# Loading the first group's wq and wo from GpSimd instead of SyncE in a decode-attention and gated-MLP forward and backward kernel

## The chip, the cores and the metric

The kernel runs on one core of one Trainium2 chip. The metric is the device time of one launch in microseconds (us): the median of three runs of the kernel before is 722.63 us (722.57 to 722.94). 0.2% of that is 1.45 us. The profile was taken in another execution, of 722.74 us, whose recorded span is 721.0 us; times below are counted from the start of that span.

The engines are named as in the profile: PE (matrix products; PEld its weight loads), DVE (vector), ACT (scalar), POOL (GpSimd) and SP (SyncE, which only issues transfers here). A small q behind a name (SPq, POOLq) is that engine's own instruction queue.

## The reference

One token x of 640 features is normalised and goes through two branches that are added to it: attention over 32 heads of 128 with a cache of 8192 keys and values per head, and a gated MLP of width 1728. The kernel returns the output and the gradients of x, both caches and all five weight matrices. The arithmetic is light; the caches and their gradients are not.

```python
q = xn @ wq                                    # 32 heads of 128
p = softmax(q . k * 128 ** -0.5);  o = p . v   # per head, 8192 positions
out = x + o @ wo + (silu(xn @ w1) * (xn @ w3)) @ w2
# and, for grad_out: d x, d k_cache, d v_cache, d wq, d wo, d w1, d w3, d w2
```

For one query, the gradient of V of a head is an outer product of the probabilities and a row of `grad_out @ wo.T`, and that of K an outer product of the score gradients and q. So each head reads 2 MB of K and 2 MB of V and writes as much back.

## The kernel before, in words

**Slots.** Ten SBUF buffers of 2 MB (`free_slots`) hold the caches. K and V of a head are loaded into two of them, PE transposes the data (L402), ACT copies the transposes out of PSUM (L404), PE forms scores (L423) and weighted sums (L517), and DVE overwrites the buffer in place with the gradient (L550, two halves of 2.28 us each). SP then stores it (`store`, L561 to L567), returns the buffer to the list and calls `load_next` (L137), which issues the next pending K or V load on SP. From L176 on it does so only when three buffers are in the list, so that a load goes into a buffer whose store was issued two stores earlier. Four of the ten buffers hold the MLP's weights until the MLP has run, between heads 1 and 2 (L910 to L913).

**Order.** The scheduling is manual: every engine runs its instructions in the order in which the program emits them, and waits on semaphores. All K and V traffic and the loads of the MLP's weights lie in SP's queue (q1 in the profile); transfers that GpSimd issues lie in another (q0). The two queues share the same 16 DMA engines.

**Groups.** Four heads share a group of weights: `wq_g` (640 rows of 512 columns, 640 KB; 1 KB runs) and `wo_g` (512 rows of 640, 640 KB; 1280-byte runs). Groups 1 and 2 are loaded by GpSimd after heads 0 and 1 (L915 to L917), the later ones after an older group is finished (L615). Only group 0 is loaded by SP (L145, L147), ahead of K and V of head 0.

**What needs group 0.** After the layer norm (L242 to L252), `prep_q(0)` (L279) multiplies xn with `wq_g` on PE (L283), ACT scales the row (L286), PE and ACT turn it into a column (`prep_qc`, L288 to L294), and `first_half` (L303) spreads it into the weight tile `qz` (L307 to L314). On PE the first transposes of head 0 (`T(0,"K",0)`, L903) stand behind these, and what forms scores needs `qz`. DVE reduces `wo_g` against `grad_out` in four steps (`prep_do`, L271 to L277), which `first_do` (L316) takes up in the middle of head 0, behind all transposes of K and two of V. The layer norm itself needs constants that DVE derives from `ident_f`, the identity that GpSimd makes at L179 (`make_identity`); the first of them, `ident_bf` at L181, stands ahead of the others in DVE's order.

**MLP.** At L910 the outer products of head 1 and then `mlp()` run. It stores its weight gradients through GpSimd (L705 to L757) and gives its buffers back; loads of K and V of heads 5 and 6 go into them, so these loads wait for GpSimd's stores.

Of the kernel before, what the change touches and what calls it, by code (L numbers as in the profile page):

```python
# [21 lines left out]
def kernel(  # L22
# [22 lines left out]
    nc = tc.nc  # L45
# [71 lines left out]
    def load_wq(g, eng):  # L117
        wq_g = wpool.tile([P, NC, GW], BF16, name="wq_g", tag="wq_g")
        eng.dma_start(wq_g[:], wq_v[:, :, g * GW:(g + 1) * GW])
        grp[g] = dict(wq=wq_g)  # L120

    def load_wo(g, eng):
        wo_g = wpool.tile([P, GH, D], BF16, name="wo_g", tag="wo_g")
        eng.dma_start(wo_g[:], wo_v[:, g * GH:(g + 1) * GH, :])
        grp[g]["wo"] = wo_g

    def load_group(g, eng):
        load_wq(g, eng)
        load_wo(g, eng)
# [7 lines left out]
    def load_next():  # L137
        if not pending or len(free_slots) < lag[0]:
            return
        kind, h = pending.pop(0)  # L140
        t = free_slots.pop(0)
        (fifo if h == 0 else fifo_wide)(t[:], (kc if kind == "K" else vc)[h])
        kv_tiles[(kind, h)] = t

    load_wq(0, nc.sync)  # L145
    load_next()
    load_wo(0, nc.sync)  # L147
    for _ in range(3):
        load_next()
    mC = free_slots.pop(0)  # L150
    mD = free_slots.pop(0)
# [836 lines left out]
```

## Time and profile before

| | |
|---|---|
| median of 3 runs | 722.63 us (722.57 to 722.94) |
| the profiled execution | 722.74 us, span 721.0 us |
| moved by DMA | 303.55 MB, mean 421 GB/s |
| read, written in HBM | 151.34 MB, 152.91 MB |
| SP's queue (q1), GpSimd's queue (q0) | 276.39 MB, 26.31 MB |
| busy: PE, PEld | 602.7 us, 378.1 us |
| busy: DVE, ACT, POOL | 471.9 us, 365.0 us, 86.0 us |
| mean granted PE clock | 0.93 |

Busy time is the sum of what an engine's instructions took. A row of the timeline gives start, duration, engine, source line, operation, output and inputs, and in brackets how long the engine was idle before it and what ended that. A row of a table by windows gives for each stretch its length, the busy time and number of instructions of each engine, then the granted PE clock, the mean busy share of the DMA engines (a little over 1 where two packets overlap, since a packet counts where it starts) and the rate. A row of the waits gives the waiting engine and line, what released it, the total, the number of waits and the longest. The chain of waits goes back from the last instruction to whatever released each step.

### The profile page before, as it was taken

To read this page: it belongs to the slowest core of one execution; us is meant where nothing else is said; L and a number is where in the kernel's file an instruction comes from. 1 tells how busy PE (TensorE), PEld (TensorE's weight loads), DVE (VectorE), ACT (ScalarE), POOL (GpSimd) and SP (SyncE) were. 2 spreads that over 40 slices of the span, in tenths; PEclk is the share of its full clock that TensorE was granted. 3 is DMA by queue.
4 is the path that set the end of the run, shared out by engine and by line. 5 is a ranking of instruction groups with operands and counts; after the bars stand their busy time and mean duration, and the time that the engine had idled before them with its cause. 6 is when DMAs were issued, how large, how long until landed. Compare 5 with 4: busy or idle time off the path is not lost.

```text
span 721.0 us, 13224 instructions
## 1 busy us (share of the span) xinstructions
PE 602.7 (84%) x5244; PEld 378.1 (52%) x5244; DVE 471.9 (65%) x895; ACT 365.0 (51%) x726; POOL 86.0 (12%) x86
## 2 busy tenths in 40 slices
PE   6989699987999989978986899878988889978931
PEld 4557566645565556545554565445554555545510
DVE  4369927678858886767745765556765666667581
ACT  3641166653566566545554556445654456545510
POOL 0110100000001112111121211111201101111110
PEclk9987999998999999999999999899998999999965
DMA  9999999999999999999999999999999999999996
GB/s 355 405 414 418 436 435 414 430 436 423 422 430 423 429 431 424 421 433 430 423 423 426 427 430 431 418 428 428 437 417 428 429 428 430 427 432 425 427 430 290
DMA packets 23163, 303.55 MB, mean 421 GB/s; under 512 B 3814, under 2 KB 5164, under 8 KB 9916
## 3 DMA queue, kind: packets, MB, share of 16 engines
q1 hardware_dynamic: 16600, 276.39, 90.1%
q0 software_dynamic: 6496, 26.31, 9.1%
q8 instruction: 41, 0.67, 0.4%
q14 instruction: 22, 0.18, 0.1%
q10 hardware_dynamic: 4, 0.00, 0.0%
HBM read 151.34 MB, written 152.91 MB: 422 GB/s over the span
## 4 chain that ended last, share of the span: by engine, by line
DMA 43%; PE 40%; DVE 10%; ACT 3%; issue 2%; SPq 0%; ACTq 0%; DVEq 0%
DMA kv<-in_A_k_cache_dram 24%; PE pT L402 19%; DMA kv<-in_A_v_cache_dram 14%; PE sA L423 5%; DVE kv L550 4%; PE dA L423 4%; DMA out_dram<-kv 4%; PE X L517 4%; PE m L440 2%; ACT KT L404 2%; DMA out_dram<-rel,rel_idx 1%; PE gu_ps L644 1%; PE dh_ps L655 1%; PE pT L283 1%; PE dx_acc L742 1%
## 5 line engine op out<-in xcount | busy, mean ns | idle before, releaser
L404 ACT COPY KT<-pT 128x512 f32<-128x512 f32 x512 | 288.5, 588 | 234.6 <-PE pT L402 212.7
L402 PE MATMUL pT<-ident_f,kv 128*128 128x128 f32 x2048 | 305.9, 288 | 54.3 <-DMA kv<-in_A_k_cache_dram 42.2
L402 PEld LDWEIGHTS pT<-ident_f,kv 128*128 128x128 f32 x2048 | 235.2, 148 | 144.2 <-PE pT L402 53.3
L550 DVE TENSOR_TENSOR kv<-qd,U 128x4096 bf16<-128x4096 bf16 x64 | 146.0, 2283 | 0.0
L550 DVE TENSOR_TENSOR kv<-qd,P 128x4096 bf16<-128x4096 bf16 x64 | 143.6, 2284 | 0.0
L517 PE MATMUL X<-kv,Z 128*32 128x512 bf16 x1024 | 97.0, 414 | 1.8 <-DVE Z L534 1.8
L423 PE MATMUL dA<-KT,qz 128*32 128x512 bf16 x512 | 85.3, 413 | 0.0
L423 PE MATMUL sA<-KT,qz 128*32 128x512 bf16 x512 | 81.5, 398 | 0.0
L370 POOL DMA_INDIRECT out_dram<-wq_g,row_idx x30 | 43.7, 1458 | 286.1 <-DMA out_dram<-wq_g,row_idx 110.4
L500 DVE SCALAR_TENSOR_TENSOR U<-m,P 128x64 bf16<-128x64 f32 x32 | 7.5, 234 | 98.8 <-PE m L440 98.8
L517 PEld LDWEIGHTS <-Z 128*32 128x32 bf16 x1024 | 33.1, 102 | 36.6 <-issue 10.4
L423 PEld LDWEIGHTS <-qz 128*32 128x32 bf16 x1024 | 29.5, 95 | 41.2 <-issue 38.4
L440 PE MATMUL m<-selc,KT 64*128 64x64 f32 x256 | 29.9, 238 | 7.5 <-ACT KT L430 7.5
L440 PEld LDWEIGHTS m<-selc,KT 64*128 64x128 f32 x256 | 21.0, 140 | 28.7 <-ACT KT L430 19.2
L370 POOL DMA_INDIRECT out_dram<-rel,rel_idx x12 | 15.5, 1292 | 138.6 <-DVE rel L596 47.6
L466 DVE TENSOR_REDUCE mrow<-m 128x1 f32<-128x64 f32 x32 | 7.1, 222 | 37.5 <-PE m L440 37.3
L460 ACT CAST qd<-pT 128x256 bf16<-128x256 f32 x32 | 11.9, 373 | 38.2 <-DVE kv L550 30.4
L473 DVE TENSOR_REDUCE negM<-m 128x1 f32<-128x128 f32 x32 | 9.3, 291 | 32.2 <-PE m L470 32.2
L274 DVE SCALAR_TENSOR_TENSOR side<-wo_g,g_bc 128x640 bf16<-128x640 bf16 x32 | 26.2, 819 | 2.3 <-DMA wo_g<-in_A_wo_dram 2.0
L602 DVE SCALAR_TENSOR_TENSOR wq_g<-wq_g,side 128x512 bf16<-128x512 bf16 x40 | 27.3, 682 | 0.0
L532 DVE SCALAR_TENSOR_TENSOR U<-m,P 128x128 bf16<-128x128 f32 x32 | 11.4, 355 | 15.8 <-PE m L530 15.8
L430 ACT COPY KT<-dA 64x512 f32<-64x512 f32 x32 | 18.6, 581 | 5.0 <-PE dA L423 5.0
(179 smaller groups left out, 403.0 us busy)
## 6 DMA issues: line engine op xcount, KB each, us to landing
out_dram<-kv SPq DMA_DIRECT2D x64, 2048.0 KB, 29.8
kv<-in_A_k_cache_dram SPq DMA_DIRECT2D x32, 2048.0 KB, 26.6
kv<-in_A_v_cache_dram SPq DMA_DIRECT2D x32, 2048.0 KB
out_dram<-wo_g POOLq DMA_DIRECT2D x8, 640.0 KB, 15.3
wq_g<-in_A_wq_dram POOLq DMA_DIRECT2D x7, 640.0 KB, 15.7
wo_g<-in_A_wo_dram POOLq DMA_DIRECT2D x7, 640.0 KB, 22.5
kv<-in_B_w_dram SPq DMA_DIRECT2D x2, 1728.0 KB
out_dram<-kv POOLq DMA_DIRECT2D x2, 1728.0 KB, 30.7
```

Of the source, the lines that this page charges most:

```text
L274: nc.vector.scalar_tensor_tensor(junk[:], G_["wo"][:, hh, :], 1.0, g_bc[:], ALU.mult, ALU.mult, accum_out=G_["do"][:, hh:hh + 1])
L370: nc.gpsimd.indirect_dma_start(dwq_row, bass.IndirectOffsetOnAxis(ap=idx, axis=0), src, None, element_offset=g * GW, bounds_check=(D - 1) ...
L402: nc.tensor.transpose(pT[:, k * P:(k + 1) * P], W3[:, 4 * c + k, :], ident_f[:])
L404: nc.scalar.copy(KT[:].rearrange("p k w -> p (k w)"), pT[:])
L423: nc.tensor.matmul(S_[kind][q:q + QW, :], lhsT=S_["qz"][:, o:o + QW], rhs=KTb[c][:, par, :], start=(c0 == 0 and par == 0), stop=(c0 == NCH ...
L430: nc.scalar.copy(XS[0:QH].rearrange("p k w -> p (k w)"), S_.pop(kind)[0:QH, :])
L440: nc.tensor.matmul(S_["m"][:, b0:b0 + 4 * J].rearrange("p (x c k t) -> p k x c t", x=4, k=4, t=2)[:, k], lhsT=XS[0:QH, k, :], rhs=selc[0:Q ...
L460: nc.scalar.copy(qd[:].rearrange("p a d -> p (a d)"), hd[h].pop("ps_r"))
L517: nc.tensor.matmul(xg["X"][q:q + QW, :], lhsT=Z[:, o:o + QW], rhs=W[:, N4 * i:N4 * (i + 1)], start=(slot == 0 and i < 4), stop=(slot == NS ...
L532: nc.vector.scalar_tensor_tensor(S_["U2"][:], S_["V"][:, 0:J].unsqueeze(2).to_broadcast([P, J, 2]), S_["m"][:, OC + NS:OC + NS + 1], S_["P ...
L550: nc.vector.tensor_tensor(dst[:, lo * DH:hi * DH].rearrange("p (j a b) -> p j a b", a=DH // 2, b=2), vec.rearrange("p (a b) -> p a b", b=2 ...
L602: nc.vector.scalar_tensor_tensor(wq_g[:, ci, :], wq_g[:, ci, :], 1.0, dqb, ALU.mult, ALU.mult, accum_out=dxa[:, ci, g:g + 1])
```

## The change

The loads of group 0 go from SP's queue to GpSimd's, and are GpSimd's first instructions, ahead of `make_identity`. SP begins with K and V of heads 0 and 1. Nothing else is changed; the same bytes are loaded into the same tiles.

```diff
-    load_wq(0, nc.sync)
-    load_next()
-    load_wo(0, nc.sync)
-    for _ in range(3):
+    load_group(0, nc.gpsimd)
+    for _ in range(4):
         load_next()
```

In the built programs SP has 139 instructions in place of 141 and POOL 65 in place of 63; PE, DVE and ACT have the same instructions in the same order.

## The prediction

> **What bounds the kernel now.** I read the page's slices and queues first, then the chain of waits, then what SP waits for.
>
> ```profile
> DMA  9999999999999999999999999999999999999996
> GB/s 355 405 414 418 436 435 414 430 436 423 422 430 423 429 431 424 421 433 430 423 423 426 427 430 431 418 428 428 437 417 428 429 428 430 427 432 425 427 430 290
> ...
> q1 hardware_dynamic: 16600, 276.39, 90.1%
> q0 software_dynamic: 6496, 26.31, 9.1%
> ...
> DMA 43%; PE 40%; DVE 10%; ACT 3%; issue 2%; SPq 0%; ACTq 0%; DVEq 0%
> ```
>
> The DMA engines are busy in every slice, and the two queues' packets fill 90.1 + 9.1 = 99.2% of the span. The same bytes can't be moved in much less time, so the kernel is bound by transfers. The chain of waits seems to disagree, with half of it on PE and DVE. In order of time it runs through PE and DVE from 12.01 to about 300 us and through transfers afterwards. So until 300 us PE never waits for data, and the early stages decide whether a late PE is felt. SP's waits tell:
>
> ```profile
> SPq L111 <- DMA out_dram<-kv: 485.8, 56, 14.1
> SPq L106 <- DVE kv L550: 72.6, 14, 10.5
> ```
>
> SP's loads wait for stores to land, which is the DMA waiting for itself, six times longer than its stores wait for DVE. A store of 2,048 KB lands 29.8 us after its issue (median, table of issues), while moving it takes 2.097 MB / 425 GB/s = 4.9 us: some 25 us of other work lies ahead of it. That queue is the cover for anything that makes the engines late.
>
> The start, by windows of 1 us (the last two columns are DMA share and GB/s) and by timeline:
>
> ```profile
> 2.00:3.00 1.00, 0.37 (x6) 0.29 (x6) 0.79 (x4) 0.82 (x1) 0.00 (x0) 1.00 0.72 228
> 3.00:4.00 1.00, 0.57 (x2) 0.48 (x2) 0.36 (x3) 0.00 (x0) 0.00 (x0) 1.00 1.01 313
> 4.00:5.00 1.00, 0.59 (x2) 0.50 (x2) 0.03 (x2) 0.26 (x1) 0.00 (x0) 1.00 1.07 338
> ...
> 6.80 2.29 PE L283 MATMUL pT<-wq_g,xn_col_bf 128*128 128x512 bf16 x5 [2.12 <-DMA wq_g<-in_A_wq_dram]
> ...
> 12.01 3.60 PE L402 MATMUL pT<-ident_f,kv 128*128 128x128 f32 x16 [0.90 <-DMA kv<-in_A_k_cache_dram]
> 13.58 0.82 DVE L274 SCALAR_TENSOR_TENSOR side<-wo_g,g_bc 128x640 bf16<-128x640 bf16 x1 [1.99 <-DMA wo_g<-in_A_wo_dram]
> ```
>
> Transfers begin a little after 2 us. wq, alone in the queue, lands 6.0 us after its issue and PE starts on it at 6.80; K of head 0 arrives at 12.0 and wo at 13.6.
>
> **The change, part by part.**
>
> 1. *The weights arrive later.* The loads of wq and wo that POOL already issues for groups 1 and 2 are the nearest rows. Up to 130 us the three loads of wq_g take 6.0 / 10.8 / 15.7 us to land (min, median, max; the 6.0 is SP's), and POOL's two of wo_g 15.2 and 21.3. All of POOL's share the engines with a full SP queue, as the changed ones will. POOL would issue wq at 0.74 us, where its identity begins now, and wo 1.05 us later (the length of POOL's first such issue). So wq lands at 0.74 + 10.8 = 11.5 to 0.74 + 15.7 = 16.4, and wo at 1.79 + 15.2 = 17.0 to 1.79 + 21.3 = 23.1; with the page's median for all seven loads of wo, 22.5, at 24.3. I take wq at 12.5: it lies nearer the 10.8, which went beside MLP weights in packets of about 14 KB, since K and V of head 0 go in 16 KB packets, and the 15.7 partly beside 32 KB ones.
>
> The Trainium skill ("DMA: Bandwidth & Descriptors", Queues, rings and completion order) says that each DMA engine takes turns between its queues, packet by packet. The trace agrees: the same 640 KB take 6.0 us alone and 10.8 beside a full queue. Another rule of that page (Anatomy of one DMA) gives a GpSimd transfer 2.0 us and its bytes at 436 GB/s; as an estimate from that page, wq would take 3.5 us and land at 4.2. By that rule the first point costs nothing, the next cover being point 2. The rows of 10.8 and 15.7 speak against it; it holds for a queue without rivals.
>
> 2. *The identity comes later.* POOL's issues took 1.05 and 0.79 us, so everything on DVE behind L181 and the layer norm shift by 1.8 us: its last step goes from 5.53 to 7.4 us. wq at 11.5 or later hides that. Without this cover PE would start on wq at 7.6 instead of 6.80, which K's arrival at 12.0 still hides but for a few tenths.
>
> 3. *Head 0 starts later.* From PE's start on wq (6.80) to the end of the L307 products (11.11) is 4.3 us of dependent steps, then the transposes follow. With wq at 12.5 they start at 16.8 in place of 12.0: 4.8 us late. Bounds: 11.5 + 4.3 = 15.8, so 3.8; 16.4 + 4.3 = 20.7, so 8.7. wo needs 3.6 us more on DVE (13.58 to 17.22) before `first_do`, which PE reaches at 20.84 now and at 25.6 then. With wo at 17.0 to 23.1 DVE is done at 20.6 to 26.7, so this adds at most 1.1; with 24.3, 27.9 - 20.84 = 7.1 in all. I take 5 us, within 3.8 to 8.7. Behind PE everything of heads 0 and 1 and of the MLP is late by this: stores, POOL's gated loads of groups 1 and 2, and the MLP's stores.
>
> 4. *What the lateness costs: nothing, under this cover.* The first store (V of head 0) is issued at 37.09 and lands at 67.1, where the next load waits for it. At that moment the stores of K (46.15) and V of head 1 (53.34) are the queue; they land at 72.7 and 79.2, as the next two loads, issued at 72.67 and 79.19, show. A store issued 15 us later would still find the queue full. The tightest place comes later. The load at 123.97 (K of head 6) waits for POOL's last big MLP store, issued at 87.63. SP's queue then holds V's load of head 5 and V's store of head 2 (110.34), which land at about 127 and 131.7 by the trace's landings. A load's first bytes move about 1.5 us after its issue (0.74 to 2.2 at the start). So this load may be 131.7 - 124.0 - 1.5 = 6.2 us late before SP's queue runs dry. The 5 us are inside. Later, from 130 to 230 us, SP's stores wait for DVE 28.8 us in all, but the DMA share by windows of 5 us stays at 0.93 or more, so the queue isn't dry there either; after 230 the stores find DVE done (0.8 us).
>
> 5. *What the transfers gain.* Now 640 KB in 1 KB runs move at 313 and 338 GB/s (3 to 5 us) against some 425 in the long run: (425 - 313) + (425 - 338) = 199 KB, 0.47 us; from 2.28 to 3.0, 306 - 228 = 78 KB, 0.18 us; around wo (9 to 13 us: 286, 379, 543, 379) 113 KB, 0.27 us. Sum 0.9 us at most, if K and V run at the full rate there. Against it: where POOL's loads of group 1 mix with SP's queue, 30 to 45 us, the rates are 417, 398 and 383, mean 399, a loss of up to 15 x 26 = 390 KB, 0.9 us; with group 2 (50 to 70 us) 415, some loss too, partly of other origin. So 0 to 0.9 gained; I take the middle, 0.5 us.
>
> **Sum.** 722.74 - 0.5 + 0 = 722.2 us for an execution such as the profiled one. Its 722.74 are the span of 721.0 and 1.7 around it, and lie 0.1 above the median of 722.63, so this is 0.1% below. A difference under 0.2%, 1.45 us, is about what a measurement can't tell from no change.
>
> **Rivals.**
>
> - *The lateness outlasts the queue* (slower). Place: the load of K of head 6 behind POOL's MLP store. It decides from 6.2 us of lateness; the price is what lies above. At the upper bound of 8.7 it is 2.5 us: 722.2 + 2.5 = 724.7. For: 15.7 is the median over POOL's seven loads of wq. Against: once SP's queue is dry, the store it waits for gets the engines alone and lands sooner. Chance 0.10.
> - *Engines set the pace after all* (slower). If the chain of waits is right up to 300 us, nothing absorbs the 5 us: 722.7 + 5 = 727.7. For: 40% of that chain on PE. Against: DMA at 9 in every slice. Chance 0.10.
> - *The transfers gain more* (faster). From 25 to 30 us the rate is 338, a shortfall of 5 x 87 = 435 KB, 1.0 us. If two queues keep the engines fed there too, the gain is 0.9 + 1.0 = 1.9: 720.8. Against: POOL's queue is empty again by then. Chance 0.13.
> - *No cost and no gain beyond noise*: my forecast, 722.2, own range 721.2 to 723.6. Chance 0.67.
>
> The range takes in the faster rival and the first slower one with its bounds, 720.7 to 725.2; the second slower one stays out. Faster by over 0.2%: 0.13; within: 0.67; slower: 0.20.
>
> **What would show it.** Of the profile after: PE's first row of L283 at 11.5 to 16.4 us and the first transposes 4.3 later, with the layer norm done before; the first store issued about 42 instead of 37; the load behind it still at 67; DMA shares near 1 around 125 to 135 us; the chain in transfers at the end. The prediction is wrong if the DMA share sinks below 0.9 between 40 and 140 us, or if the lateness at the first store is still there in the last one (issued at 696.3 now).

## The result, and the profile after

| | before | after |
|---|---|---|
| median | 722.71 us (10 runs) | 724.62 us (10 runs) |
| ratio after / before | | 1.0024, 95% interval 1.0014 to 1.0033 |
| profiled execution, its span | 722.74 us, 721.0 us | 724.26 us, 722.5 us |

The change makes the kernel 0.24% slower, about 1.7 us. The prediction had 722.2 and a gain too small to measure. The page of the kernel after, the same lines as before:

```profile
DMA  9999999999999999999999999999999999999996
GB/s 361 396 422 419 434 423 418 430 427 420 413 420 435 419 426 438 420 420 432 422 429 429 423 428 431 421 425 432 428 423 426 424 430 430 429 428 429 426 427 293
...
q1 hardware_dynamic: 15416, 275.08, 89.7%
q0 software_dynamic: 6816, 27.62, 9.6%
...
DMA 42%; PE 41%; DVE 10%; ACT 3%; issue 2%; SPq 0%; POOL 0%; ACTq 0%; DVEq 0%; POOLq 0%
```

Nothing here looks like a loss. The DMA engines are again busy in every slice, and 89.7 + 9.6 = 99.3% of a longer span is filled with packets. The same bytes took the engines longer. Where, the windows tell (first two rows: before; last column GB/s):

```profile
60.00:130.00 70.00, 61.97 (x572) 41.49 (x570) 50.60 (x108) 30.86 (x64) 3.86 (x7) 0.95 1.01 429
130.00:210.00 80.00, 70.27 (x611) 44.04 (x610) 60.31 (x162) 44.26 (x89) 5.29 (x9) 0.96 1.00 425
```

```profile
60.00:130.00 70.00, 62.11 (x621) 43.47 (x622) 52.18 (x108) 26.02 (x55) 3.85 (x7) 0.88 1.01 426
130.00:210.00 80.00, 70.61 (x588) 44.38 (x583) 59.55 (x159) 42.31 (x86) 5.29 (x9) 0.91 1.00 420
```

From 60 to 210 us the rate is 3 to 5 GB/s lower, at the same DMA share. Ahead of that (393 before, 395 after) and behind it (427 in both, 210 to 700 us) it isn't. Counting the bytes of finished packets in the two traces gives the same: at 60 us the kernel after is 0.4 us ahead, at 130 us 0.15 behind, at 210 us 1.3 behind, at 700 us 1.5 behind. So the time isn't lost in the first microseconds, where the change was made, but between 60 and 210 us, and nearly all of it before a third of the span is over.

What the change did at the start, in the timeline after; under it stand two rows of the kernel before and one more of the kernel after:

```profile
1.31 1.01 POOL L119 DMA_DIRECT2D wq_g<-in_A_wq_dram  x1 [0.86 <-POOLq L970]
2.31 0.79 POOL L124 DMA_DIRECT2D wo_g<-in_A_wo_dram  x1
...
7.90 0.17 DVE L250 CAST xn_col_bf<-xn_col 128x5 bf16<-128x5 f32 x1
...
15.64 2.29 PE L281 MATMUL pT<-wq_g,xn_col_bf 128*128 128x512 bf16 x5 [8.60 <-DMA wq_g<-in_A_wq_dram]
...
19.88 3.68 PE L400 MATMUL pT<-ident_f,kv 128*128 128x128 f32 x16
...
29.65 0.23 PE L305 MATMUL pT<-cb,ident_bf 128*64 128x4 bf16 x4 [0.17 <-DVE cb L275]
```

```profile
20.84 0.23 PE L307 MATMUL pT<-cb,ident_bf 128*64 128x4 bf16 x4
...
37.09 16.58 SPq L106 DMA_DIRECT2D out_dram<-kv  x3
```

```profile
45.90 9.41 SPq L106 DMA_DIRECT2D out_dram<-kv  x2
```

wq lands 14.3 us after its issue, at 15.6 us, and PE has stood idle for 8.6 us. The transposes start at 19.88 instead of 12.01, 7.9 us late. `first_do` (the row at 29.65, before at 20.84) is 8.8 us late. It waits for wo, which takes 23.6 us, but PE stands idle for it only 0.17 us; most of the added 0.9 us is PE's work between the two rows, which took 0.7 us longer. The first store goes out at 45.90 instead of 37.09, again 8.8.

SP's queue shows what this lateness does (waits of the kernel after, whole span; then the issues around its longest wait):

```profile
SPq L111 <- DMA out_dram<-kv: 401.3, 46, 14.8
SPq L106 <- DVE kv L548: 139.9, 23, 17.8
```

```profile
164.22 0.34 SPq L106 DMA_DIRECT2D out_dram<-kv  x1
164.66 0.96 SPq L111 DMA_DIRECT2D kv<-in_A_v_cache_dram  x1
183.47 0.34 SPq L106 DMA_DIRECT2D out_dram<-kv  x1
183.91 0.47 SPq L111 DMA_DIRECT2D kv<-in_A_k_cache_dram  x1
```

SP's waits for DVE have doubled (72.6 to 139.9 us), and its waits for stores to land have sunk by 84.5 us: the queue is shorter. The longest, 17.8 us, ends with the store of V of head 5, behind `rel_setup`, a table set-up of some 10 us on DVE and PE ahead of head 6. Call *backlog* the bytes that are issued and not yet moved, worked out from the issues and packets of a trace every 0.5 us. At 183 us it is down to 1.6 MB, less than one transfer of K or V; before, it never fell under 6.1 MB between 178 and 230 us.

### The profile page after: what moved, and what is told of

It is laid out like the page before. It is cut to its first block, busy times and chain, and to the rows that moved or that the text cites. A ratio compares the mean times of both kernels' runs of the same rounds, so it can differ in the third digit from the quotient of the medians.

```text
span 722.5 us, 13218 instructions
## 1 busy us (share of the span) xinstructions
PE 599.5 (83%) x5237; PEld 376.4 (52%) x5244; DVE 471.8 (65%) x895; ACT 362.5 (50%) x726; POOL 87.0 (12%) x88
## 3 DMA queue, kind: packets, MB, share of 16 engines
q1 hardware_dynamic: 15416, 275.08, 89.7%
## 4 chain that ended last, share of the span: by engine, by line
DMA 42%; PE 41%; DVE 10%; ACT 3%; issue 2%; SPq 0%; POOL 0%; ACTq 0%; DVEq 0%; POOLq 0%
PE pT L400 19%; DMA kv<-in_A_k_cache_dram 14%; DMA out_dram<-kv 13%; DMA kv<-in_A_v_cache_dram 11%; PE sA L421 5%; PE dA L421 4%; DVE kv L548 4%; PE X L515 4%; DMA wo_g<-in_A_wo_dram 3%; PE m L438 2%; ACT KT L402 2%; PE gu_ps L642 1%; PE dh_ps L653 1%; ACT KT L428 1%; PE dx_acc L740 1%
## 5 line engine op out<-in xcount | busy, mean ns | idle before, releaser
L400 PE MATMUL pT<-ident_f,kv 128*128 128x128 f32 x2048 | 302.5, 286 | 38.4 <-DMA kv<-in_A_k_cache_dram 23.6
L400 PEld LDWEIGHTS pT<-ident_f,kv 128*128 128x128 f32 x2048 | 232.8, 147 | 129.5 <-PE pT L400 53.6
L515 PE MATMUL X<-kv,Z 128*32 128x512 bf16 x1024 | 95.0, 407 | 1.8 <-DVE Z L532 1.8
L421 PE MATMUL sA<-KT,qz 128*32 128x512 bf16 x512 | 83.9, 408 | 0.0
L421 PE MATMUL dA<-KT,qz 128*32 128x512 bf16 x512 | 82.4, 401 | 0.0
L488 DVE RECIPROCAL rZ<-m 128x1 f32<-128x1 f32 x32 | 5.3, 166 | 22.3 <-PE m L482 22.3
## 6 DMA issues: line engine op xcount, KB each, us to landing
wo_g<-in_A_wo_dram POOLq DMA_DIRECT2D x8, 640.0 KB, 23.6
```

The source lines that it names most:

```text
L400: nc.tensor.transpose(pT[:, k * P:(k + 1) * P], W3[:, 4 * c + k, :], ident_f[:])
L421: nc.tensor.matmul(S_[kind][q:q + QW, :], lhsT=S_["qz"][:, o:o + QW], rhs=KTb[c][:, par, :], start=(c0 == 0 and par == 0), stop=(c0 == NCH ...
L515: nc.tensor.matmul(xg["X"][q:q + QW, :], lhsT=Z[:, o:o + QW], rhs=W[:, N4 * i:N4 * (i + 1)], start=(slot == 0 and i < 4), stop=(slot == NS ...
```

## The experiments

Two theories stood at first. **L**: the lateness of head 0 is the cause, wherever it comes from. **S**: the start of the queues is (K's cold first packets, and two queues that take turns). Lateness below is the issue of the first store, against 37.09 us.

**Lateness without moving a load: late4, late9, late14, late_eq.** The kernel before, with DVE held up in the layer norm by fills of a tile that is zero already:

```diff
+    for _ in range(N):                       # 13, 22, 33; 16 and a half in late_eq
+        nc.vector.memset(acc[:], 0.0)
     nc.vector.tensor_copy(xn_col_bf[:], xn_col[:])
```

> The same with 13 fills, about 4.4 us of lateness, less than the 6.2 us that the prediction gave as the point from which lateness costs. Theory L with a cost in proportion: 0.8 us slower, 723.5. Theory L with a threshold: no change, 722.7. Theory S: no change.

> The kernel before, all loads where they were, with 22 more vector fills of 0.49 us each (of a PSUM tile that is filled with the same zeros already) ahead of the last step of the layer norm, so that head 0's transposes start about 8.8 us late, as in the changed kernel. Theory L (the lateness of head 0 alone makes the transfers between about 100 and 210 us slower): 1.5 to 1.9 us slower than before, about 724.3, with the bytes moved falling behind between 100 and 210 us. Theory S (the loss comes from the start of the queues: K's first packets of 1.18 us, and GpSimd's queue alternating with SyncE's): no change, 722.7.

> The same with 33 fills, about 14 us of lateness. Theory L in proportion: 2.6 us slower, 725.3; with a threshold near 6 us: up to 8 us slower if the engines set the pace from there. Theory S: no change, 722.7.

> The kernel before with 16 and a half fills, sized from the two runs with 13 and 22 so that V of head 0 is stored about 8.8 us late, exactly as in the changed kernel, with all loads left in SyncE's queue. Theory L (lateness alone): 1.3 to 2.1 us slower than before, as the change. Theory S (the queues' start): under 0.5 us slower.

The fills took 0.48 us each, but each waited for the one before and began 0.67 us after it, so the runs are later than meant: 6.3, 12.8, 20.0 and 9.8 us. Two rows of late_eq show the delay and the first store; PE waits for DVE, while wq had landed at 6.5 us:

```profile
16.62 2.31 PE L286 MATMUL pT<-wq_g,xn_col_bf 128*128 128x512 bf16 x5 [11.94 <-DVE xn_col_bf L255]
...
46.89 9.41 SPq L106 DMA_DIRECT2D out_dram<-kv  x2
```

Measured ratios: late4 1.0017 (1.0008 to 1.0026), late_eq 1.0025 (1.0016 to 1.0034), late9 1.0075 (1.0058 to 1.0091), late14 1.0177 (1.0163 to 1.0192). That is 1.2, 1.8, 5.4 and 12.8 us on 722.7. With all loads where they were, 9.8 us of lateness cost what the change costs with 8.8. S predicted no loss, or under 0.5 us, in each of the four, and falls as the explanation of these losses. From late_eq to late9 the time rises by 3.6 us for 3.0 of lateness, and to late14 by 7.4 for 7.2: from about 9 us on, every microsecond is paid in full. At 6.3 and 8.8 us the loss is 1.2 and 1.7, with intervals that overlap. late4, meant to lie below the prediction's 6.2 us, came out just at it.

In late14 the queue does run dry; windows of 5 us (last columns: DMA share, GB/s):

```profile
50.00:55.00 5.00, 5.00 (x60) 3.02 (x54) 3.11 (x6) 2.35 (x5) 1.97 (x3) 1.00 0.62 235
55.00:60.00 5.00, 5.00 (x40) 3.16 (x40) 4.27 (x2) 3.91 (x8) 0.00 (x0) 1.00 0.97 366
60.00:65.00 5.00, 5.00 (x48) 2.87 (x49) 2.23 (x6) 3.20 (x7) 0.00 (x0) 1.00 0.55 236
65.00:70.00 5.00, 2.37 (x34) 1.20 (x26) 3.08 (x7) 0.85 (x2) 1.71 (x3) 0.99 0.62 262
```

That is what I had looked for as the sign of a loss. In the kernel after no such window exists: between 30 and 700 us its lowest share in 5 us is 0.88.

**Halves of the change: split, wq_pool, order.**

```diff
 split:                      wq_pool:                    order:
+    load_wq(0, nc.sync)    +    load_wq(0, nc.gpsimd)  +    load_next()
+    load_wo(0, nc.gpsimd)  +    load_next()            +    load_wq(0, nc.sync)
+    for _ in range(4):     +    load_wo(0, nc.sync)    +    load_next()
+        load_next()        +    for _ in range(3):     +    load_wo(0, nc.sync)
                            +        load_next()        +    for _ in range(2):
                                                        +        load_next()
```

> wq of group 0 stays first in SyncE's queue, wo alone goes to GpSimd as its first work. wq lands near 6.8 us as before, K of head 0 earlier than 11.9, wo by about 18; head 0 at most 1 to 2 us late through wo. Theory L: within 0.4 us of before, 722.3 to 723.1. Theory S: part of the loss is still there, about 723.5.

> Half of the change: wq of group 0 alone goes to GpSimd, as its first work; SyncE's queue is K, wo, V of head 0 and so on. wq lands at about 14 to 16, head 0 starts about 8 us late through wq alone, wo is early. Theory L (the lateness costs, however it comes about): 1.0 to 2.0 us slower than before. If GpSimd's wo is what costs: under 0.5 us slower.

> The other half of the change alone: SyncE's queue begins with K of head 0, then wq, V of head 0, wo; nothing goes to GpSimd. wq lands after K, at about 9, so head 0 starts some 2 us late, and wo behind V at about 14 to 18. Theory L: no change, 722.4 to 723.1, since lateness below about 6 us is covered. Theory S (a start with K costs): about 724.

split: 1.0008 (0.9999 to 1.0017), 2.4 us late: no clear loss (1.2 us at most), though wo took 13.4 us to land there: GpSimd's queue does little harm where little waits for it. wq_pool: 1.0016 (1.0007 to 1.0025), 1.2 us. wq alone seems to bring most of the loss, though the intervals overlap. It took 10.7 us to land there (with wo in SP's queue) and head 0 was only 4.7 us late, not the 8 I expected. Its bytes are 0.1 us ahead at 60 us and 1.1 behind at 140, so they are lost later and not at the start: lateness costs below the 6.2 us that the prediction gave as the point from which it does.

order: 1.0043 (1.0030 to 1.0056). Here both theories missed. It is 4.7 us late, as wq_pool, and nothing goes to GpSimd, but it loses 3.1 us. In its profiled execution (span 723.4, 2.4 us over) the bytes moved are 0.4 us behind at 60 us, 1.5 at 140 and 1.9 at 700. The middle part is what wq_pool loses too (1.1 us behind at 140). The first 0.4 us belong to the start: with wq's 1 KB packets between K and V the rate at 8 to 11 us was 321 to 344 GB/s. Its timed runs spread from 724.71 to 727.97 us and the profiled one (725.18) lies near their lower end.

**One place or many: after_rel8, before_rel8.** The set-up that stands ahead of head 6 is moved ahead of head 8, in the kernel after and, as a control, in that before.

```diff
-        if h == 6:
+        if h == 8:
             rel_setup()
```

> The changed kernel, with the table set-up that runs ahead of head 6 (rel_setup, some 10 us of DVE and PE work in which no gradient is stored) moved ahead of head 8. Theory P (the place where the lateness meets an almost empty queue is the store of V of head 5, behind that set-up): most of the loss goes, within 0.8 us of before, 722.3 to 723.5; the bytes moved no longer fall behind at 190 to 200 us. Theory Q (the lateness costs everywhere between 100 and 210 us, with no single place): 724.3 as the change.

> The control for the last: the kernel before with the set-up ahead of head 8. Its queue held 12 us of work at that place, so both theories say no change, 722.7 within 0.4; if it gains more than that, the place costs the kernel before as well.

after_rel8: 1.0017 (1.0009 to 1.0026), 1.2 us; the control 1.0001 (0.9992 to 1.0010). The backlog at 178 to 230 us is back to 5.4 MB, and yet by the medians only about a third of the loss is gone; the intervals of the two ratios overlap, so even that isn't certain. In its trace the bytes moved are 0.3 us behind at 130 us, 1.1 at 150 and 1.5 at 700, as far as in the kernel after. Theory P, one decisive place, finds no support: relieved at head 6, the kernel still pays at an earlier one, between 115 and 150 us. How much is paid where is less certain: up to head 6 the two changed kernels run the same instructions, and their traces still differ by 0.5 us at 150 us (0.5 and 1.1 behind).

**GpSimd's load without a rival: alone.** SP's first load waits until wq has landed; the identity is made ahead of this copy (not shown).

```diff
+    nc.gpsimd.tensor_copy(free_slots[0][:, 0:1], grp[0]["wq"][:, 0, 0:1])
     for _ in range(4):
         load_next()
```

> The changed kernel, but SyncE's first load waits until wq has landed (a one-column copy on GpSimd from wq into K's buffer, which K then overwrites), so that GpSimd's wq has no rival in the DMA engines. If a shared queue is what makes it take 14.3 us, it lands 3.5 to 6 us after its issue here. Head 0 is then 2 to 3 us late through K instead; the DMA engines stand idle for 1 to 2 us before K, which goes straight into the time: 723.5 to 725.

The timeline of alone:

```profile
1.30 1.01 POOL L119 DMA_DIRECT2D wq_g<-in_A_wq_dram  x1 [0.86 <-POOLq L971]
...
5.93 0.18 POOL L148 COPY kv<-wq_g 128x1 bf16<-128x1 bf16 x1 [2.25 <-DMA wq_g<-in_A_wq_dram]
...
8.13 2.31 PE L282 MATMUL pT<-wq_g,xn_col_bf 128*128 128x512 bf16 x5 [1.08 <-DVE xn_col_bf L251]
```

wq lands 4.6 us after its issue, against 14.3 beside K and V. So it is mostly the shared engines that make it late, not GpSimd. The packets tell how. In the kernel after wq's first packet starts 4.7 us after the issue, against 1.7 in alone; then its 160 packets of 4 KB take turns with 156 of 16 KB from SP's queue, from 5.96 to 14.5 us, where in alone they need 2.3 us. PE then waits for the layer norm (8.13), as the prediction's second step said of the case without its cover. The time is 1.0048 (1.0033 to 1.0064), 3.5 us, more than the 0.8 to 2.3 that I expected: SP begins only at 6.14 us, at 10 us the bytes moved are already 1.7 us behind, and this is never recovered.

**Lateness and backlog.** The smallest backlog in two stretches, worked out from each trace (late14 is left out, its queue runs empty):

| run | late by, us | time lost, us (ratio - 1, times 722.7) | backlog 100 to 150 us, MB | 178 to 230 us, MB |
|---|---|---|---|---|
| before | 0 | | 2.5 | 6.1 |
| before_rel8 | 0.1 | 0.1 | 2.3 | 7.2 |
| split | 2.4 | 0.6 (0 to 1.2) | 2.1 | 5.5 |
| alone | 2.6 | 3.5, in part at the start | 2.1 | 5.6 |
| order | 4.7 | 3.1, in part at the start | 1.4 | 3.9 |
| wq_pool | 4.7 | 1.2 | 1.6 | 3.5 |
| late4 | 6.3 | 1.2 | 1.6 | 2.5 |
| after_rel8 | 8.6 | 1.2 | 2.0 | 5.4 |
| after | 8.8 | 1.7 | 1.9 | 1.6 |
| late_eq | 9.8 | 1.8 | 1.6 | 1.2 |
| late9 | 12.8 | 5.4 | 1.3 | 0.7 |

Apart from alone, the runs that go down to 2.0 MB or less in the first stretch have a clear loss, and those that keep 2.1 or more have none. That is no threshold yet: split (2.1) and after_rel8 (2.0) lie side by side, and the intervals of their losses overlap. At 2 MB the engines still have work: idle engines, counted from packets, cost nothing between 60 and 230 us in the kernels before, after and late4, 0.4 us in late_eq and 0.6 in late9. What grows is the length of packets. Of K's and V's 32 KB load packets between 60 and 640 us, most take 1213 ns; over 1363 ns took 26 of 3494 before and 74 of 3484 after, 45 of the 48 added ones between 118 and 208 us. There are 17 in before_rel8, 23 in split, 52 to 69 in late4, alone, order, after_rel8 and wq_pool, 101 in late_eq and 167 in late9. Summed over the 16 engines, all load packets of 32 KB took 302.9 us per engine before and 304.8 after, 1.9 more, and the 16 KB ones 0.7 more, while wq and wo took 0.6 less. Sums and place fit the loss. But the slow packets don't sit where the backlog is smallest. Of the 53 in the kernel after between 118 and 208 us, none started with under 2 MB of backlog, 5 with 2 to 4, 39 with 4 to 6 and 9 with more; before, none of the 100 that started under 6 MB between 60 and 640 us was slow. So thin queues and slow packets go together from run to run, but the one isn't shown as the cause of the other, and what makes the packets slow stays open.

## Why the prediction was wrong, step by step

- *What bounds the kernel*: right. The transfers set the time; the second slower rival, engines all the way (727.7), did not come about at 8.8 us of lateness; only what exceeds some 9.8 us is paid in full.
- *Step 1, the arrival of the weights*: the size failed. I took 12.5 us for wq and it was 15.6, inside the 11.5 to 16.4. Two parts: POOL's first issue began at 1.31 and not 0.74, and it took 14.3 us, nearer the 15.7 than the 10.8 that I chose. wo, at 25.9, came after both of my bounds (23.1 and 24.3). The sentence on the Trainium skill ("DMA: Bandwidth & Descriptors", Anatomy of one DMA: 2.0 us and the bytes at 436 GB/s, so 3.5) was to hold for a queue without rivals: there 4.6 us were measured, 1.1 more than the estimate, and 14.3 with a rival.
- *Step 2, the identity*: right in kind. The layer norm ended at 8.1 instead of 5.7 us, 2.4 late and not 1.8, well hidden by wq.
- *Step 3, the lateness*: 8.8 us where I took 5, just over my upper bound of 8.7. wq brings 7.9 of it (15.64 plus the 4.2 of dependent steps is 19.88); the other 0.9 the sum didn't have: 0.7 of longer work on PE and 0.2 for wo.
- *Step 4, the price of lateness*: this is the step that failed and turned the sign. I put it at nothing, and it was about 1.7 us. "Nothing, under this cover" was tested only against a queue that runs dry. Two things were wrong. First the measure: the loss begins at 4.7 us of lateness or less, while all engines are still busy and about 1.6 MB are issued and not moved (wq_pool). Secondly the place: runs do lose around K's load of head 6, which I priced (123.97 before; 121.38 after, earlier although the MLP store that it waits for was issued 8.8 us later, since that store landed in 25.0 us and not in 36.3). But I waved through the stretch from 130 to 230 us because its DMA share was near 1 *before*. That the queue isn't dry in the old profile doesn't say how much lateness it can take: V's store of head 5 had 12.5 us of backlog ahead of it at 174 us, 8.8 of which the change used up. The signs that I had named were blind to this: the share in 5 us never sank below 0.91 between 40 and 140 us, and of the 8.8 us at the first store 2.1 were left at the last (698.4 against 696.3).
- *Step 5, the gain of the transfers*: not shown as such. The kernel after is 0.4 us ahead at 60 us, where I had 0.5, but late4, late_eq and late9 are 0.5 to 0.7 ahead there with all loads where they were, so that agreement is luck. By the packets wq and wo cost the engines 0.6 us less through GpSimd; K's first packets, slow on idle engines, took back 0.4.
- *The rivals*: the lateness that outlasts the queue, 724.7 at a chance of 0.10, came nearest. The median is 724.6. That the number fits is in part luck: it was made of 2.5 us above a point of 6.2, and at 4.7 us 1.2 were lost already. Its mechanism was half right: no queue outlasted, but one worn thin, in two places.

## What to carry to other kernels

Where transfers bound a kernel and the engines run behind a full queue, the slack of an early step is less than the smallest backlog anywhere later. How much less isn't shown; here 4.7 us cost something where the smallest backlog was 2.5 MB, about 5.9 us at 425 GB/s. Look for it place by place, and add the lateness before looking. A small load that starts the dependent chain belongs ahead of the large ones in one queue: here a second queue didn't run beside the first but took turns with it, and 640 KB that land in 6.0 us at the head of SP's queue took 14.3 us beside it. A DMA share near 1 is no proof that nothing is lost.

## What the runs showed of the hardware that I had not expected

- The same 1 KB runs of wq move in packets of 1024 B (median 46 ns, 640 of them) when SP issues them and of 4096 B (160 ns, 160 of them) when GpSimd does; for the engines the latter is a little cheaper, 2.09 us each in place of 2.25.
- The first twelve 16 KB packets of K in the kernel after, on idle engines, took 967 to 1429 ns against 611 later on.
- Transfers lost speed before they ran out of work. In the kernel after 46 of the 491 32 KB load packets that started with under 6 MB issued and not moved took over 1363 ns (up to 2302, usually 1213), of the other 2993 only 28; the DMA share was 0.88 to 1.10 in windows of 5 us between 115 and 210 us. A small backlog alone isn't enough: before, it was none of 100.
